# Block-sparse attention and feed-forward on one core: three score banks instead of two, and squares kept in their place

## The chip, the cores and the metric

One core of a Trainium2 chip runs the kernel. Its engines work side by side: PE multiplies matrices, DVE, ACT and POOL work on vectors, and SP issues the transfers. The metric is the time of one execution in microseconds.

## What is computed

Attention with 4 batches, 8 heads, 768 positions and 64 numbers per head, followed by a feed-forward layer on the 3072 tokens that come out of it:

```python
scores = scale * np.matmul(q, k.transpose(0, 1, 3, 2))
mask = np.abs(blk_i - blk_j) <= window          # blocks of 32
mask = mask | (blk_i == 0) | (blk_j == 0) | (blk_i == n_blocks - 1) | (blk_j == n_blocks - 1)
...                                             # and three sampled blocks for each block of q
scores = np.where(mask, scores, -1000000000.0)
attn = np.exp(scores - np.max(scores, axis=-1, keepdims=True))
attn = attn / (np.sum(attn, axis=-1, keepdims=True) + 1e-09)
x = np.matmul(attn, v)                          # tokens x 512
h = x @ w_in                                    # 512 -> 2048
out = np.maximum(0.01 * h, h) @ w_out           # 2048 -> 512
```

Since each block of q sees at most twelve blocks of keys (two blocks of q together), the kernel gathers these keys and values and computes 384 scores per row.

## The kernel before

The work is cut into 192 units: twelve items (batch b and pair of query tiles j), in each four groups of queries k and four pairs of heads hp. A tile of the unit 3, 2, 1, 0 is named s_3_2_1_0, and so on. A unit goes through this chain. PE multiplies q by the gathered keys into a PSUM bank s (line 651), DVE adds the mask and takes the extreme into mx (658), ACT takes the exponential (669), DVE makes the reciprocal r of the sums (677, 678), ACT writes the high fp16 half of the weights into pp (684), DVE the low half (689), SP issues the transpose of pp into pt (692), PE multiplies pt by the gathered values vg into the bank av (714), and ACT, DVE and POOL turn that into the input x of the feed-forward (721 to 732). pp and pt have six buffers each.

The feed-forward is cut into 96 chunks. For each, 24 matmuls fill a bank h (749), ACT (756) and DVE (760) read it, and DVE and POOL write g (765, 766). Twelve matmuls multiply g by the second weight into the bank o (779), ACT writes ob (797), and SP issues the output (808). The bank h is free again once DVE's line 760 has read it.

Queries and keys are split into high and low halves before use. prep_q squares a tile of q on ACT (523) with a sum per row, one small matmul of PE adds the rows up (126, q_sum), DVE makes the scale, ACT writes the high half of qa (530), DVE the low one (532), SP issues the transpose into qs (535), and two copies of it with the two halves of the partitions swapped into qxs (537, 538). The load of the next q into the single buffer rq is line 473. prep_k does the same for keys (494, 126, 506, 508, transpose 512); from the second batch on, the four head pairs of a batch share one buffer k16, so that the square of a pair writes where the transpose of the pair before still reads.

The gathered values vg are copied from DRAM by SP: one copy of 128 rows (611) and six of 32 rows (621), whose addresses SP loads and computes first (619). All transfers of the kernel, loads, transposes, gathers and outputs, are issued on SP, in one order.

PSUM has eight banks: two for s, three with the tag h (these also hold the small sums), one for av, two for o.

The main loop goes through the units, and the letters of a string set in which order the pieces of work of a step are written. A scheduler then orders the instructions of each engine by priority. The priority is a running number; the helper together lowers it for all but the first matmul of a group, so that a group stays in one piece. Scores are written one step ahead, for two units at once when the first of a pair of units is done (the setting spair), and the second unit of the pair comes first on PE. An instruction without a late priority can be placed ahead of others on its engine as soon as the scheduler believes its inputs to be there; the squares of prep_q and prep_k and their matmuls are such.

Of the kernel before, what the change touches and what calls it, by code (L numbers as in the profile page):

```python
# [13 lines left out]
F32 = mybir.dt.float32  # L14
# [5 lines left out]
P = 128  # L20
# [9 lines left out]
CFG = {  # L30
    "ahead": 3,
    "av_lag": 3,
    "bs": 1500,
    "early": 2,
    "flag": 1,
    "g": 2,
    "g_at": 0,
    "ht": 1,
    "k_at": 6,
    "k_at0": 26,  # L40
# [10 lines left out]
    "rk": 2,  # L51
    "rmax": 1.0,
    "rmin": 0.0,
    "side": 1.2,
    "side0": 1.6,
    "spair": 1,
    "spread": 8,
    "v_at": 28,
    "wr": [(0, 1.0), (4, 3.0), (10, 4.0), (18, 4.5)],
# [6 lines left out]
def tile_block_sparse_attention_ffn(  # L66
# [19 lines left out]
    nc = tc.nc  # L86
# [20 lines left out]
    pa = ctx.enter_context(tc.tile_pool(name="pa", bufs=2))  # L107
    pf = ctx.enter_context(tc.tile_pool(name="pf", bufs=2))
    dr = ctx.enter_context(tc.tile_pool(name="dr", bufs=2, space=bass.MemoryType.DRAM))
    ps_s = ctx.enter_context(tc.tile_pool(name="ps_s", bufs=2, space=bass.MemoryType.PSUM))  # L110
    ps_o = ctx.enter_context(tc.tile_pool(name="ps_o", bufs=2, space=bass.MemoryType.PSUM))
    ps_1 = ctx.enter_context(tc.tile_pool(name="ps_1", bufs=1, space=bass.MemoryType.PSUM))

# [1 line left out]
    nc.vector.memset(zero, 0.0)  # L115

    def bank(name, tag="h"):
        return ps_1.tile([P, 512], F32, tag=tag, name=name, bufs={"h": 3, "av": 1}[tag])


    ones = cst.tile([P, P], F32, name="ones")
# [2 lines left out]
    def scale_sum(ss, n, name):  # L124
        pb = bank(f"{name}_sum")
        nc.tensor.matmul(pb[:, :n], ones, ss, start=True, stop=True)
        return pb

    def scale_of(pb, n, name, total=False, keep=None, fl="q"):

        pool, tg = (sm, "sc") if keep is None else (cst, keep)
        m = 1 if total else n
        tot = sm.tile([P, 4], F32, tag=f"tot{fl}", name=f"{name}_tot")
        if total:
            nc.vector.tensor_reduce(out=tot[:, :1], in_=pb[:, :n], op=ALU.add, axis=AX.X)
            nc.vector.tensor_scalar(out=tot[:, :1], in0=tot[:, :1], scalar1=TINY, scalar2=None, op0=ALU.max)
        else:
            nc.vector.tensor_scalar(out=tot[:, :m], in0=pb[:, :m], scalar1=TINY, scalar2=None, op0=ALU.max)  # L140
        ex = sm.tile([P, 4], I32, tag=f"ex{fl}", name=f"{name}_ex")
        nc.vector.tensor_scalar(
            out=ex[:, :m], in0=tot[:, :m].bitcast(I32), scalar1=24, scalar2=23,
            op0=ALU.logical_shift_right, op1=ALU.logical_shift_left,
        )
        inv = pool.tile([P, 4], F32, tag=f"{tg}_i", name=f"{name}_inv")
        s = pool.tile([P, 4], F32, tag=f"{tg}_s", name=f"{name}_s")
        nc.vector.tensor_scalar(out=inv[:, :m], in0=ex[:, :m].bitcast(F32), scalar1=2.0 ** 50, scalar2=None, op0=ALU.mult)
        nc.vector.reciprocal(out=s[:, :m], in_=inv[:, :m])
        return inv, s  # L150
# [3 lines left out]
    def scales(ss, n, name, **how):  # L154
        now = tc.cur_priority
        tc.cur_priority = now - CFG["bs"]
        begin = len(nc.cur_bb.bb.instructions)
        pb = scale_sum(ss, n, name)
        loose.update(i.name for i in nc.cur_bb.bb.instructions[begin:])
        r = scale_of(pb, n, name, **how)  # L160
        tc.cur_priority = now + 8
        return r

    def together(emits):

        now = tc.cur_priority
        begin = len(nc.cur_bb.bb.instructions)
        for n, emit in enumerate(emits):
            if n == 1:
                tc.cur_priority = now - 100000  # L170
            emit()
        new = nc.cur_bb.bb.instructions[begin:]
        for i in new[1:]:
            tc.add_manual_dep(i, new[0].name, mybir.DependencyInfo(
                mybir.DependencyClass.NoSync, mybir.DependencyReason.DATA), reason="together")
        tc.cur_priority = now + len(new)
# [40 lines left out]
    def build_masks():  # L217
# [8 lines left out]
        for r in range(NR):  # L226
# [9 lines left out]
            pattern=[[-1, NB - 2], [0, NR]], base=-1, channel_multiplier=1,  # L236
            compare_op=ALU.is_equal, fill=0.0)
        pm = bank("mask_ps")[:, :(NT - 1) * 2 * NR].rearrange("p (t a r) -> p t a r", t=NT - 1, a=2)
        for a in range(2):
            sel = sels[a]  # L240
# [244 lines left out]
    def prep_k(b, hp, rk):  # L485

        nm = f"k{b}_{hp}"
        ss = sm.tile([P, 1], F32, tag="ssk", name=f"ss_{nm}")
        if b == 0:
            k16 = early_k.bitcast(F16)[:, (NP + hp) * 2 * S:(NP + hp + 1) * 2 * S].rearrange(  # L490
                "p (n l d) -> p n l d", n=HC, l=2)
        else:
            k16 = pa.tile([P, HC, 2, D], F16, tag="k16", name=f"k16_{nm}", bufs=1)
        nc.scalar.activation(flat(k16)[:, :S], flat(rk), AF.Square, accum_out=ss)
        yield 1.0
        yield 0.01
        pb = scale_sum(ss, 1, nm)
        yield 0.2
        inv, s = scale_of(pb, 1, nm, fl="k")
        if (b, "inv") not in kready:  # L500
            kready[b, "inv"] = cst.tile([P, NP], F32, name=f"kinv_{b}")
        nc.vector.tensor_scalar(
            out=kready[b, "inv"][:, hp:hp + 1], in0=inv[:, :1], scalar1=-SCALE, scalar2=None, op0=ALU.mult)
        yield 0.4
        raw = rk.rearrange("p h c d -> p (h c) d")
        nc.scalar.activation(k16[:, :, 1, :], raw, AF.Copy, scale=s[:, :1])
        yield 1.0
        nc.vector.scalar_tensor_tensor(
            out=k16[:, :, 0, :], in0=raw, scalar=s[:, :1], in1=k16[:, :, 1, :], op0=ALU.mult, op1=ALU.subtract)
        if b not in kts:  # L510
            kts[b] = pa.tile([P, H, S], F16, tag="kt", name=f"kt_{b}", bufs=2)
        nc.sync.dma_start_transpose(
            out=kts[b][:, 2 * hp:2 * hp + 2, :].rearrange("p h (c t) -> p (h c) t", t=P),
            in_=k16.rearrange("p n l d -> p (n l d)"))
        kready[b, hp] = True
        yield 1.2

    def prep_q(b, j, i, rq):

        nm = f"q{b}_{j}_{i}"  # L520
        ss = sm.tile([P, 1], F32, tag="ssq", name=f"ss_{nm}")
        qa = pa.tile([P, H, 2, D], F16, tag="qa", name=f"qa_{nm}", bufs=1)
        nc.scalar.activation(flat(qa)[:, :H * D], rq.rearrange("p h d -> p (h d)"), AF.Square, accum_out=ss)  # L523
        yield 0.7
        yield 0.01
        pb = scale_sum(ss, 1, nm)
        yield 0.2
        inv, s = scale_of(pb, 1, nm)
        yield 0.4
        nc.scalar.activation(qa[:, :, 1, :], rq, AF.Copy, scale=s[:, :1])  # L530
        yield 0.7
        nc.vector.scalar_tensor_tensor(
            out=qa[:, :, 0, :], in0=rq, scalar=s[:, :1], in1=qa[:, :, 1, :], op0=ALU.mult, op1=ALU.subtract)
        qs = pa.tile([P, H, P], F16, tag="qs", name=f"qs_{nm}", bufs=2)
        nc.sync.dma_start_transpose(out=qs, in_=flat(qa))
        qxs = pa.tile([P, H, P], F16, tag="qxs", name=f"qxs_{nm}", bufs=2)
        nc.sync.dma_start(out=qxs[:D], in_=qs[D:])
        nc.sync.dma_start(out=qxs[D:], in_=qs[:D])
        qstack[b, j, i] = (qs, qxs, inv)
        yield 0.8  # L540
# [157 lines left out]
    def pair_av(pr):  # L698

        if pr.hp == 0:  # L700
            avs[pr.item.n, pr.T] = bank(f"av_{pr.nm}", "av").rearrange("p (n l t) -> p n l t", n=NP, l=2)
        pr.av = avs[pr.item.n, pr.T]
        for u in pr.units:
            require_v(u.b, u.hp, u.T)
        emits = []
        for u in pr.units[::-1]:
            n = NCH * u.parts
            for c in range(n):
                for l in range(2):
                    for hh in range(2):  # L710
                        vt = vgs[u.b, u.T][:, c, 2 * u.hp + hh, :] if u.T else v16s[u.b, u.hp][:, c, hh, :]
                        emits.append(lambda o=pr.av[hh * D:(hh + 1) * D, u.hp], a=vt[:, l * D:(l + 1) * D],
                                     m=u.pt[c // NCH][:, :, c % NCH, hh * D:(hh + 1) * D], c=c, l=l, n=n:
                                     nc.tensor.matmul(o, a, m, start=(c == 0 and l == 0), stop=(c == n - 1 and l == 1)))  # L714
        together(emits)

    def tile_evac(pr):

# [93 lines left out]
    for b in range(B):  # L812
        for j in range(NI):
# [3 lines left out]
            for k_ in range(TPI):  # L817
                for hp in range(0, NP, 2):
                    pr = Unit()
# [30 lines left out]
    def require_v(b, hp, T):  # L850
        until(("v", b), lambda: (b, hp) in v16s if T == 0 else (b, "ready") in scr)
        while T and (b, T) not in vgs:
            start_gather_v()
# [173 lines left out]
    for u in units:  # L1027
        it, ui = u.item, u.k * NP + u.hp
        b, nb = it.b, it.b + 1
# [161 lines left out]
```

## Time and profile before

| what | time, us |
|---|---|
| median of three runs | 949.08 |
| lowest and highest | 946.14 and 949.32 |
| the profiled execution | 946.47 |
| its span | 944.7 |
| PE busy in it | 754.8 |
| DVE busy | 609.1 |
| ACT busy | 488.1 |
| POOL busy | 331.3 |

The profile counts an engine as busy while it computes. SP computes nothing, so it does not stand in this table; what it does is seen in its timeline, where each row is the time during which SP worked on issuing transfers. A wait in the list of waits is idle time of an engine ahead of an instruction, put down to the instruction or transfer that came last. Windows give the busy time of each engine in a stretch and the clock that was granted to PE.

### The profile page before, as it was taken

To read this page: it belongs to the slowest core of one execution; us is meant where nothing else is said; L and a number is where in the kernel's file an instruction comes from. 1 tells how busy PE (TensorE), PEld (TensorE's weight loads), DVE (VectorE), ACT (ScalarE), POOL (GpSimd) and SP (SyncE) were. 2 spreads that over 40 slices of the span, in tenths; PEclk is the share of its full clock that TensorE was granted. 3 is DMA by queue.
4 is the path that set the end of the run, shared out by engine and by line. 5 is a ranking of instruction groups with operands and counts; after the bars stand their busy time and mean duration, and the time that the engine had idled before them with its cause. 6 is when DMAs were issued, how large, how long until landed. Compare 5 with 4: busy or idle time off the path is not lost. (4 is left out here: it accounts for less than half of the span.)

```text
span 944.7 us, 21784 instructions
## 1 busy us (share of the span) xinstructions
PE 754.8 (80%) x7020; PEld 492.8 (52%) x7020; DVE 609.1 (64%) x1643; ACT 488.1 (52%) x1063; POOL 331.3 (35%) x469
## 2 busy tenths in 40 slices
PE   1325456788978979979897968989888988989998
PEld 1214334465645645646554635556455655656674
DVE  4989899996857667557565565567466655745221
ACT  4565768575535456456455554456355554535121
POOL 0234665542215344243324242333323433532221
PEclk9998557799989989999999998999999999989999
DMA  9996798678685767766675978676785665555200
GB/s 209 283 276 162 162 244 187 164 148 167 141 180 128 160 121 157 160 137 130 151 165 111 171 134 147 151 146 127 151 161 125 137 136 139 120 113 123 32 23 23
DMA packets 336624, 139.38 MB, mean 148 GB/s; under 512 B 299389, under 2 KB 311678, under 8 KB 336510
## 3 DMA queue, kind: packets, MB, share of 16 engines
q1 hardware_dynamic: 336510, 137.99, 68.5%
q8 instruction: 55, 0.90, 0.4%
q14 instruction: 59, 0.48, 0.2%
HBM read 65.57 MB, written 12.58 MB: 83 GB/s over the span
## 5 line engine op out<-in xcount | busy, mean ns | idle before, releaser
L779 PE MATMUL o<-W,g 128*128 128x512 f16 x1152 | 279.1, 388 | 7.6 <-ACT ob L797 2.9
L749 PE MATMUL h<-x,W 128*128 128x256 f16 x2304 | 280.9, 279 | 0.3 <-DVE ht L760 0.3
L749 PEld LDWEIGHTS <-W 128*128 128x128 f16 x2304 | 227.2, 101 | 50.7 <-issue 10.5
L766 POOL TENSOR_TENSOR g<-ht,g 128x512 f16<-128x512 f32 x96 | 115.3, 1201 | 336.5 <-DVE g L765 201.2
L689 DVE SCALAR_TENSOR_TENSOR pp<-p,r,pp 128x384 f16<-128x384 f32 x208 | 142.5, 702 | 106.0 <-ACT pp L684 104.4
L779 PEld LDWEIGHTS <-g 128*128 128x128 f16 x1152 | 108.8, 100 | 137.4 <-issue 23.9
L669 ACT ACTIVATE p<-p,mx 128x384 f32<-128x384 f32 x208 | 125.8, 606 | 96.3 <-DVE mx L658 67.0
L591 POOL COPY kg<-kt 128x256 f16 x264 | 129.3, 510 | 131.6 <-PE s L651 74.9
L684 ACT ACTIVATE pp<-p,r 128x384 f16<-128x384 f32 x208 | 119.6, 607 | 103.9 <-DMA pt<-pp 72.0
L714 PE MATMUL av<-pt,vg 128*64 128x128 f16 x2112 | 83.0, 231 | 50.5 <-DMA pt<-pp 40.3
L658 DVE CUSTOM_DVE_ANT_0 p<-s,em,nsc 128x384 f32<-128x384 f32 x176 | 101.9, 609 | 21.1 <-PE s L651 20.0
L714 PEld LDWEIGHTS <-vg 128*64 128x64 f16 x2112 | 72.1, 116 | 77.0 <-issue 57.4
L760 DVE SCALAR_TENSOR_TENSOR ht<-h,gd,ht 128x512 f32<-128x512 f32 x80 | 59.8, 747 | 56.0 <-ACT ht L756 55.7
L756 ACT ACTIVATE ht<-h,gs 128x512 f32<-128x512 f32 x80 | 54.0, 675 | 63.9 <-PE h L749 48.7
L651 PE MATMUL s<-kg,qs_q 128*64 128x384 f16 x352 | 65.1, 364 | 12.1 <-DVE mx L658 7.7
L732 POOL TENSOR_TENSOR x<-xf,x 128x256 f16<-128x256 f32 x48 | 35.8, 745 | 90.7 <-ACT x L730 90.0
L651 PE MATMUL s<-kg,qxs_q 128*64 128x384 f16 x352 | 63.9, 357 | 4.3 <-DMA qxs_q<-qs_q 4.3
L651 PEld LDWEIGHTS <-qs_q 128*64 128x64 f16 x416 | 27.9, 116 | 68.7 <-issue 45.4
L523 ACT ACTIVATE qa_q<-rq 128x512 f16<-128x512 f32 x25 | 15.7, 628 | 68.9 <-DMA rq<-in_q_dram 68.9
L765 DVE CAST g<-ht 128x512 f16<-128x512 f32 x96 | 43.4, 452 | 8.9 <-PE o L779 7.5
L677 DVE TENSOR_SCALAR sum<-sum 128x2 f32<-128x2 f32 x96 | 24.9, 259 | 37.1 <-ACT p L669 36.1
L669 ACT ACTIVATION_READ_ACCUMULATOR p<-p,mx 128x1 f32 x208 | 38.9, 187 | 0.0
(126 smaller groups left out, 726.0 us busy)
## 6 DMA issues: line engine op xcount, KB each, us to landing
vg<-scr SPq DMA_DIRECT2D x280, 64.0 KB, 1.9
vg<-scr SPq DMA_DIRECT2D x44, 256.0 KB, 3.1
v<-in_v_dram SPq DMA_DIRECT2D x32, 192.0 KB, 3.4
qxs_q<-qs_q SPq DMA_DIRECT2D x48, 128.0 KB, 3.0
scr<-v SPq DMA_DIRECT2D x16, 384.0 KB, 3.7
W<-in_moe_w_in_dram SPq DMA_DIRECT2D x5, 1024.0 KB, 5.9
rq<-in_q_dram SPq DMA_DIRECT2D x20, 256.0 KB, 3.5
out_dram<-ob SPq DMA_DIRECT2D x20, 256.0 KB, 2.3
```

What stands on the lines that cost most here:

```text
L591: nc.gpsimd.tensor_copy(out=kg[:, :, slot * BLOCK:(slot + 1) * BLOCK], in_=kt[:, :, bass.ds(off, BLOCK)])
L651: nc.tensor.matmul(o, a, k, start=(n == 0), stop=(n == 1)))
L658: nc.vector.tensor_tensor_reduce(out=u.p[i], in0=u.sp[i], in1=kgs[u.b, u.T][1] if u.T else zero.to_broadcast([P, KEYS]), scale=u.nsc, scal ...
L669: nc.scalar.activation(u.p[i], u.p[i], AF.Exp, scale=-1.0, bias=u.mx[:, :1], accum_out=u.pair.sum[:, u.pi, i:i + 1])
L684: nc.scalar.activation(pp[:, 0, :], p, AF.Copy, scale=u.r)
L689: nc.vector.scalar_tensor_tensor(out=pp[:, 1, :], in0=p, scalar=u.r, in1=pp[:, 0, :], op0=ALU.mult, op1=ALU.subtract)
L714: nc.tensor.matmul(o, a, m, start=(c == 0 and l == 0), stop=(c == n - 1 and l == 1)))
L749: nc.tensor.matmul(c.ph[:, i], w, x, start=(d == 0 and m == 0), stop=(d == NP - 1 and m == 2)))
L756: nc.scalar.activation(c.t, c.ph, AF.Copy, scale=scale[1])
L760: nc.vector.scalar_tensor_tensor(out=c.t, in0=c.ph, scalar=scale[0], in1=c.t, op0=ALU.mult, op1=ALU.max)
L766: nc.gpsimd.tensor_tensor(out=c.g[:, 1], in0=c.t, in1=c.g[:, 0], op=ALU.subtract)
L779: nc.tensor.matmul(o, a, w, start=(c.first and i == 0 and m == 0), stop=(c.last and i == 1 and m == 2)))
```

## The change

Three banks instead of two for s, and two instead of three with the tag h. Scores are written for one unit at a time, in the order of the units (spair 0). And a new helper, hold, ties an instruction to the one that stands before it on the same engine in the written program, without a wait on the chip: only the order of the engine is fixed. It is applied to the square and the sum matmul of every k but those of the first batch, and of every q but the very first. A third use, for av, stays off.

```diff
+    "hold": "kq",
+    "s": 3,
-    "spair": 1,
+    "spair": 0,
-    ps_s = ctx.enter_context(tc.tile_pool(name="ps_s", bufs=2, space=bass.MemoryType.PSUM))
+    ps_s = ctx.enter_context(tc.tile_pool(name="ps_s", bufs=CFG["s"], space=bass.MemoryType.PSUM))
-        return ps_1.tile([P, 512], F32, tag=tag, name=name, bufs={"h": 3, "av": 1}[tag])
+        return ps_1.tile([P, 512], F32, tag=tag, name=name, bufs={"h": 5 - CFG["s"], "av": 1}[tag])
+    def hold(begin):
+
+        ins = nc.cur_bb.bb.instructions
+        prev = next((i for i in reversed(ins[:begin]) if i.engine == ins[begin].engine), None)
+        if prev is not None:
+            tc.add_manual_dep(ins[begin], prev.name, mybir.DependencyInfo(
+                mybir.DependencyClass.NoSync, mybir.DependencyReason.DATA), reason="hold")
...
+        begin = count()
         nc.scalar.activation(flat(k16)[:, :S], flat(rk), AF.Square, accum_out=ss)
+        if b and "k" in CFG["hold"]:
+            hold(begin)
         yield 1.0
         yield 0.01
+        begin = count()
         pb = scale_sum(ss, 1, nm)
+        if b and "k" in CFG["hold"]:
+            hold(begin)
...
+        later = (b or j) and "q" in CFG["hold"]
+        begin = count()
         nc.scalar.activation(flat(qa)[:, :H * D], rq.rearrange("p h d -> p (h d)"), AF.Square, accum_out=ss)
+        if later:
+            hold(begin)
         yield 0.7
         yield 0.01
+        begin = count()
         pb = scale_sum(ss, 1, nm)
+        if later:
+            hold(begin)
```

In the rows that follow, numbers at the end of a name are buffers' numbers, and the same statement has another line number after the change.

ACT, at the preparation of q2_1_1, whose high half is `qa_q2_1_1`. Before, the high half came five rows ahead of the square of k3_2:

```order
L506 ACTIVATE k16_k3_1_10014<-rk_3_1_9666,k3_1_s_10282 128x12x64
L684 ACTIVATE pp_2_1_1_0_0_10656<-p_2_1_1_0_0_10462,r_2_1_1_0_10647 128x384
L756 ACTIVATE ht_1_2_10_10344<-h_1_2_10_10306,gs2_2849 128x512
L669 ACTIVATE p_2_1_1_2_0_10650,sum_2_1_1_2_10658<-p_2_1_1_2_0_10650,mx_2_1_1_2_10651 128x384
L669 ACTIVATE p_2_1_1_3_0_10709,sum_2_1_1_2_10658<-p_2_1_1_3_0_10709,mx_2_1_1_3_10710 128x384
L530 ACTIVATE qa_q2_1_1_10148<-rq_2_1_1_9664,q2_1_1_s_10392 128x8x64
L684 ACTIVATE pp_2_1_1_1_0_10715<-p_2_1_1_1_0_10496,r_2_1_1_0_10647 128x384
L721 ACTIVATE avt_2_0_3_2_10678<-av_2_0_3_0_10429 128x256
L684 ACTIVATE pp_2_1_1_2_0_10771<-p_2_1_1_2_0_10650,r_2_1_1_2_10762 128x384
L730 ACTIVATE x_2_0_9710<-xf_2_0_3_2_10732 128x4x64
L494 ACTIVATE k16_k3_2_10457,ss_k3_2_10456<-rk_3_2_10113 128x768
```

And now:

```order
L524 ACTIVATE k16_k3_1_10014<-rk_3_1_9666,k3_1_s_10277 128x12x64
L709 ACTIVATE pp_2_1_1_1_0_10715<-p_2_1_1_1_0_10496,r_2_1_1_0_10642 128x384
L749 ACTIVATE avt_2_0_3_2_10678<-av_2_0_3_0_10424 128x256
L709 ACTIVATE pp_2_1_1_2_0_10766<-p_2_1_1_2_0_10645,r_2_1_1_2_10757 128x384
L758 ACTIVATE x_2_0_9705<-xf_2_0_3_2_10727 128x4x64
L784 ACTIVATE ht_1_2_10_10344<-h_1_2_10_10301,gs2_2844 128x512
L507 ACTIVATE k16_k3_2_10452,ss_k3_2_10451<-rk_3_2_10108 128x768
L709 ACTIVATE pp_2_1_1_3_0_10835<-p_2_1_1_3_0_10709,r_2_1_1_2_10757 128x384
L555 ACTIVATE qa_q2_1_1_10148<-rq_2_1_1_9664,q2_1_1_s_10392 128x8x64
```

The high half of q2_1_1 now stands two rows behind the square of k3_2, which writes where the transpose of k3_1 reads.

SP, at the same place: from the transpose of k3_1 to that of q2_1_1, before:

```order
L692 DMA_TRANSPOSE pt_2_1_0_0_0_10408<-pp_2_1_0_0_0_10340 128x6x128
L512 DMA_TRANSPOSE kt_3_10011<-k16_k3_1_10014 128x12x128
L535 DMA_TRANSPOSE qs_q2_1_1_10397<-qa_q2_1_1_10148 128x8x128
L473 DMA rq_2_2_0_10402<-in_q_dram 128x8x64
L692 DMA_TRANSPOSE pt_2_1_0_1_0_10466<-pp_2_1_0_1_0_10410 128x6x128
```

And now:

```order
L717 DMA_TRANSPOSE pt_2_1_0_0_0_10408<-pp_2_1_0_0_0_10335 128x6x128
L530 DMA_TRANSPOSE kt_3_10011<-k16_k3_1_10014 128x12x128
L717 DMA_TRANSPOSE pt_2_1_0_1_0_10461<-pp_2_1_0_1_0_10410 128x6x128
L494 DMA rk_3_3_10493<-in_k_dram 128x6x64 x2
L717 DMA_TRANSPOSE pt_2_1_0_2_0_10500<-pp_2_1_0_2_0_10463 128x6x128
L636 DMA vg0_95<-scr_2_8209 128x1024
L644 TENSOR_LOAD offs_89
L644 ISA x2
L646 ISA
L646 DMA vg0_95<-scr_2_8209 32x1024
L560 DMA_TRANSPOSE qs_q2_1_1_10397<-qa_q2_1_1_10148 128x8x128
```

Two transposes of pp, two loads of k and two copies to vg have come in between. At the last q, q3_2_1, the rows of SP (row 1465 of 1540 before, 1466 of 1541 now) have the same neighbours in the same order as before.

PE, behind the sum of the last q (row 11981 of 13879 before and now), before:

```order
L126 MATMUL q3_2_1_sum_15945<-ss_q3_2_1_15739,ones_83 128x1
L651 LDWEIGHTS qs_q3_2_0_15274
L651 MATMUL s_3_2_1_1_0_15979<-kg1_94,qs_q3_2_0_15274 64x384
L651 LDWEIGHTS qs_q3_2_0_15274
L651 MATMUL s_3_2_1_1_0_15979<-kg1_94,qs_q3_2_0_15274 64x384
L651 LDWEIGHTS qxs_q3_2_0_15276
L651 MATMUL s_3_2_1_1_0_15979<-kg1_94,qxs_q3_2_0_15276 64x384
L651 LDWEIGHTS qxs_q3_2_0_15276
L651 MATMUL s_3_2_1_1_0_15979<-kg1_94,qxs_q3_2_0_15276 64x384
L651 LDWEIGHTS qs_q3_2_0_15274
L651 MATMUL s_3_2_1_0_0_15978<-kg1_94,qs_q3_2_0_15274 64x384
```

And now:

```order
L128 MATMUL q3_2_1_sum_15945<-ss_q3_2_1_15739,ones_83 128x1
L676 LDWEIGHTS qs_q3_2_0_15274
L676 MATMUL s_3_2_1_0_0_15978<-kg1_94,qs_q3_2_0_15274 64x384
L676 LDWEIGHTS qs_q3_2_0_15274
L676 MATMUL s_3_2_1_0_0_15978<-kg1_94,qs_q3_2_0_15274 64x384
L676 LDWEIGHTS qxs_q3_2_0_15276
L676 MATMUL s_3_2_1_0_0_15978<-kg1_94,qxs_q3_2_0_15276 64x384
L676 LDWEIGHTS qxs_q3_2_0_15276
L676 MATMUL s_3_2_1_0_0_15978<-kg1_94,qxs_q3_2_0_15276 64x384
L739 LDWEIGHTS vg1_96
L739 MATMUL av_3_1_3_0_15987<-pt_3_1_3_1_0_15710,vg1_96 64x128
```

The scores of one unit stand there where those of two stood, and the first unit comes first.

## Rows read from the trace of the kernel before

**Rows 1.** Busy time by stretch: stretch, length, engines, PE clock, DMA share, GB/s.

```profile
150.00:769.00 619.00, 532.80 (x5075) 344.93 (x5073) 411.86 (x1144) 331.85 (x754) 219.37 (x332) 0.95 0.71 147
769.00:840.00 71.00, 67.94 (x660) 44.85 (x655) 44.27 (x115) 35.22 (x83) 29.41 (x45) 0.98 0.58 128
```

**Rows 2.** Timeline of SP, 759 to 776: start, length, line, operation, how many.

```profile
759.81 6.04 SPq L621 DMA_DIRECT2D vg<-scr  x6
765.95 3.90 SPq L692 DMA_TRANSPOSE pt<-pp  x3
769.94 1.26 SPq L535 DMA_TRANSPOSE qs_q<-qa_q  x1
```

**Rows 3.** Tile pp from 0 to 760 us: instructions, first and last start.

```profile
L689 DVE SCALAR_TENSOR_TENSOR pp<-p,r,pp x180: 594/618/2475, 53.0 to 759.2; 128x384 f16<-128x384 f32 x180
L692 SPq DMA_TRANSPOSE pt<-pp x175: 1209/1252/3559, 59.7 to 756.9; - x175
```

**Rows 4.** Waits, whole run (last row: 150 to 880 us): total, times, longest.

```profile
ACT pp L684 <- DMA pt<-pp: 72.0, 33, 6.8
ACT qa_q L523 <- DMA rq<-in_q_dram: 68.9, 20, 6.3
...
PE av L714 <- DMA pt<-pp: 54.7, 29, 5.3
...
PE s L651 <- DVE mx L658: 25.4, 11, 9.6
...
PE k_sum L126 <- ACT k_k L494: 20.8, 7, 4.9
...
PE s L651 <- DVE mx L658: 4.4, 5, 1.3
```

**Rows 5.** Waits of SP's own queue, whole run: three of its rows.

```profile
SPq L537 <- DMA qs_q<-qa_q: 6.1, 8, 2.3
SPq L512 <- DVE W L314: 4.5, 1, 4.5
...
SPq L535 <- DVE W L312: 3.4, 1, 3.4
```

**Rows 6.** Timelines of ACT, DVE and SP around q2_1_1, 555 to 573 us.

```profile
561.54 0.70 ACT L530 ACTIVATE qa_q<-rq,q_s 128x512 f16<-128x512 f32 x1
...
568.63 0.84 ACT L494 ACTIVATE k_k<-rk 128x768 f16<-128x768 f32 x1 [2.42 <-DMA kt<-k_k]
...
562.27 0.75 DVE L532 SCALAR_TENSOR_TENSOR qa_q<-rq,q_s,qa_q 128x512 f16<-128x512 f32 x1 [0.24 <-ACT qa_q L530]
...
563.75 1.45 SPq L512 DMA_TRANSPOSE kt<-k_k  x1
565.29 1.62 SPq L535 DMA_TRANSPOSE qs_q<-qa_q  x1
...
570.76 1.32 SPq L482 DMA_DIRECT2D rk<-in_k_dram  x1
```

**Rows 7.** Timelines of SP and PE at the last q, 836 to 850 us.

```profile
839.49 1.27 SPq L535 DMA_TRANSPOSE qs_q<-qa_q  x1
...
842.82 0.51 PE L651 MATMUL s<-kg,qs_q 128*64 128x384 f16 x3 [1.60 <-DMA qs_q<-qa_q]
845.97 0.82 PE L651 MATMUL s<-kg,qxs_q 128*64 128x384 f16 x3 [2.63 <-DMA qxs_q<-qs_q]
```

**Rows 8.** Line 749: the page's row, its share by stretch, one chunk's timelines.

```profile
L749 PE MATMUL h<-x,W 128*128 128x256 f16 x2304 | 280.9, 279 | 0.3 <-DVE ht L760 0.3
...
769.00:846.00 77.00, 28.24 (x240) 22.82 (x240) 0.97 0.59 130
...
460.04 2.76 PE L779 MATMUL o<-W,g 128*128 128x512 f16 x12
462.64 2.78 PE L749 MATMUL h<-x,W 128*128 128x256 f16 x24
...
472.51 0.74 DVE L760 SCALAR_TENSOR_TENSOR ht<-h,gd,ht 128x512 f32<-128x512 f32 x1
```

More of the change, by code (lines that the diff above doesn't have):

```diff
@@ L162, in scales @@
         return r
+    def hold(begin):
[4 more added lines that the diff above has]
+                mybir.DependencyClass.NoSync, mybir.DependencyReason.DATA), reason="hold")
+    count = lambda: len(nc.cur_bb.bb.instructions)
     def together(emits):
@@ L714, in pair_av @@
                                      nc.tensor.matmul(o, a, m, start=(c == 0 and l == 0), stop=(c == n - 1 and l == 1)))
+        begin = count()
         together(emits)
+        if pr.item.n and "a" in CFG["hold"]:
+            hold(begin)
     def tile_evac(pr):
```

## The prediction, made before the changed kernel ran

> **What bounds the kernel now.** I read the share of busy time by stretch first. Between 150 and 769 us PE is busy 532.80 of 619 us, and between 769 and 840 it is busy 67.94 of 71 us [rows 1]. A reader might stop there and call PE the bound, with some 86 us of idle time in the long middle stretch to be won by a better order. The next view, the DMA issues on SP, says otherwise. Every DMA of this kernel is issued on that one queue, and its rows lie end to end: six gathers from 759.81 for 6.04 us end at 765.85, three transposes of pp start at 765.95 and take 3.90 us, to 769.85, the transpose of qs starts at 769.94 [rows 2]. One transpose of pp holds SP for 1.252 us, and 175 of them start before 760 us [rows 3], 219 us in all; a gather step costs about 6.04/6 = 1.01 us. SP has no room in which to go faster.
>
> Whether SP or its producers are behind is told by counting. By 760 us DVE has finished 180 tiles of pp and SP has taken up 175 of them [rows 3]: five finished tiles, some 6 us of transposes, are lying in front of SP. pp has six buffers, so this is nearly as far ahead as the producers can get. Hence the large waits in the list are SP's lag seen from other engines: ACT waits 72.0 us for a transpose that would free a pp buffer, PE 54.7 us for pt, ACT 68.9 us for the next q [rows 4]. All of these end with something that SP issues.
>
> The end is set so. SP issues the transpose of the last q (q3_2_1) at 839.49; PE runs out of other scores, waits 1.60 us for it at 842.82 and 2.63 us for its swapped copy at 845.97 [rows 7], and then has work without a real pause to the end at 944.7. So the time is SP's row count up to that transpose, plus some 99 us of PE work behind it.
>
> **The change, part by part.** The sum starts from the profiled run, 946.47 us (span 944.7 and 1.8 around it). The three runs had a median of 949.08, 2.6 above this one, and it was itself near their low end.
>
> SP's own rows: the same transposes, gathers and loads. The transpose of the last q stands at row 1465 before and 1466 now, between the same neighbours, so the pace-setter has the same work ahead of the critical point: 0 us. What SP itself waits is small. It waits 6.1 us for qs ahead of the swapped copies, 4.5 and 3.4 us at the start for transposes whose tiles come behind the decoding of the weights [rows 5]; 14 us in all, the most that a new order could take from SP. The swapped copies still follow their transpose at a distance of one to six rows, so I take 0 and keep -14 for the range.
>
> Scores, one unit at a time with three banks: no matmul is added or removed. The waits that it aims at, PE's scores on DVE's read of the last bank, are 25.4 us in 11, of which only 4.4 us in 5 lie between 150 and 880 us [rows 4]; the other 21 are at the start, while SP issues loads. I put this at 0, since the freed PE would only bring pp sooner to a queue that already has five tiles lying. If that cover were missing, it is -4.4.
>
> Squares held in place (ACT and PE): a q square comes 8 to 20 rows later on ACT, so ACT waits less in front of it for its load, and the matmul behind a k square no longer stands early on PE, where such matmuls cost 20.8 us of waiting [rows 4]. Again 0 for the time, covered by SP; -20.8 without the cover. The reverse side is one place where SP itself comes to depend on ACT. At q2_1_1 the high half on ACT started at 561.54 and the low half on DVE at 562.27, ending at 563.02; SP wanted them at 565.29 [rows 6]. Now the high half stands behind the square of k3_2, and this square waits for the transpose of k3_1, issued at 563.75, to leave the buffer; it started at 568.63 [rows 6]. Add the square's 0.84, 0.7 for one pp, and 0.70 and 0.75 for the two halves: ready at about 571.6. SP reaches the moved transpose after two pt (2.5), two loads of k (1.32) [rows 6] and two copies to vg (1.5 by the gather steps): 563.75 + 1.45 + 5.3 = 570.5. So SP stands some 1.1 us, with all pt behind it: **+1.1**. It is 0 if SP is a little later there than I count, and 5.5 if ACT in front of the high half waits twice for a pp buffer as long as it does on average, 72.0/33 = 2.2 us [rows 4].
>
> Feed-forward with two banks instead of three: with three, PE waited 0.3 us for a bank in the whole run [rows 8]. A bank is free when DVE has read it. In the long case h ended at 462.64 + 2.78 = 465.42 and DVE's read at 472.51 + 0.74 = 473.25, 7.8 us later [rows 8]. With two banks the next but one product waits if PE has less than that to do between. One other h (2.78 us) and one o (2.76) make 5.5 [rows 8], so the long case costs 2.3 us. Ten products lie between 769 and 846 (240 matmuls of 24 each) [rows 8]; there PE has 1.60 + 2.63 = 4.2 us to give before it, not SP, sets the end. Earlier than 769 the five tiles in front of SP cover it. Bounds: 0 if no release is long, 10 x 2.3 - 4.2 = +19 if every one is. In the busy middle ACT and DVE also serve attention, as they do at 465; towards the end they are freer. I take two long ones, 4.6 against 4.2 of slack: **+0.4**, and use five long ones, 11.5 less 4.2 = +7.3, for the rival below and the range.
>
> The sum: 946.5 + 0 + 1.1 + 0.4 = 948.0 on the level of the profiled run. A median of several runs may lie there or, as it did before, 2.6 higher; I add 1 and forecast **949**: no change.
>
> Two rules of the Trainium skill bear on this. Its page Perfetto Trace Analysis says under What "DMA-bound" means that a kernel can be bound by the issuing engine's sequencer, which then shows solid DMA slices. The trace agrees: three groups of SP rows in a row have at most 0.10 us between them [rows 2]. By that rule a reordering of PE and ACT alone leaves 946.5. The same page asks under Matmuls that independent groups rotate through different PSUM banks, so that one's evacuation overlaps the next; taking a bank from the feed-forward goes against it, and by it the time would be the second rival's.
>
> **The rivals.** *PE sets the pace.* If the queue in front of SP were a mere consequence of bursts, PE's own waits would count: 20.8 for the k sums and 4.4 for the scores [rows 4]: 946.5 - 25.2 = 921.3, some 923 for a median. For it speaks PE's 68 of 71 us between 769 and 840; against it, SP's rows without gaps and the tiles lying in front of it at 760. Chance 0.10.
>
> *Two banks are too few.* The mechanism above with five long releases between 769 and 846: 948.0 - 0.4 + 7.3 = 955. It decides from the second long release on, where 4.2 us are used up. For it: PE is busy 96% there. Against: with three banks only one wait of 0.3 us was seen. This ends slower. Chance 0.14.
>
> *SP waits for ACT.* What I priced at 1.1 us at q2_1_1 comes at further q's too, since the high halves now stand later on ACT while SP wants them at the same place. Three more places, at each of which ACT waits its average 2.2 us for a pp buffer [rows 4] ahead of the high half: +6.6, from 948.0 to 955. It decides once a high half comes later than SP's own lag of some 6 us covers. Chance 0.11.
>
> *SP's own waits shrink.* If the start, where attention comes some rows sooner past the weight decoding, gives SP its 4.5 and 3.4, and half of the 6.1 goes: 7.9 + 3.1 = 11 less than 948.0 is 937, with the same 1 added 938. Chance 0.17.
>
> That the hold does nothing for k is possible as well: its square stays 11 to 16 rows from the transpose it waits for. It would give the forecast's time and is counted in it.
>
> **How the numbers follow.** Forecast 0.48, rivals 0.10, 0.14, 0.11 and 0.17. About 0.5% (4.7 us) is what measurement tells from no change: under 944.3 faster, over 953.8 slower. Faster 0.10 + 0.17 = 0.27, slower 0.14 + 0.11 = 0.25, same 0.48. The forecast's own range is 944.5 to 953.5. For 8 in 10 I leave out PE's pace (0.10), the lowest part of SP's waits and what lies above 958, together some 0.18: 936 to 958.
>
> **What would show it.** In the changed kernel's trace: SP's rows still end to end from 60 to 878 us; finished pp still ahead of taken ones at 760; the last q's transpose issued within 5 us of 839.5; some 99 us behind it. The score waits on DVE and the k sums' waits gone without SP moving would prove the cover; waits of h on DVE at L760's place between 769 and 846 the second rival; a semaphore wait of SP before a qs transpose the third. The forecast is wrong if SP shows gaps where before it had none, or if that transpose is issued before 834.

## The result, and the profile after

The changed kernel takes 952.08 us against 948.99 for the kernel before, in 15 runs each: a ratio of 1.0043, interval 1.0028 to 1.0057 (the ratio is worked out over all runs; the quotient of the two medians is 1.0033). Three later comparisons gave 1.0089 (1.0068 to 1.0110), 1.0058 (1.0035 to 1.0081) and 1.0061 (1.0038 to 1.0084). It is slower by 4 to 8 us. The time lies inside the forecast's range, but the forecast was no change, and that is wrong. The time lies between the forecast and the second and third rival, both at 955; what the runs show is the mechanism of neither.

The head of the page of after: span and busy time by engine.

```profile
span 949.1 us, 21876 instructions
...
PE 758.9 (80%) x7020; PEld 493.3 (52%) x7020; DVE 604.0 (64%) x1643; ACT 491.4 (52%) x1063; POOL 323.5 (34%) x469
```

PE and ACT are busy 4.1 and 3.3 us longer than before, DVE and POOL less long. The list of waits of after (total, times, longest), which answers to [rows 4]:

```profile
ACT pp L709 <- DMA pt<-pp: 84.2, 48, 4.4
...
PE av L739 <- DMA pt<-pp: 57.3, 29, 7.8
...
PE s L676 <- DVE mx L683: 25.5, 16, 6.6
...
PE s L676 <- DMA qs_q<-qa_q: 25.5, 8, 8.8
...
PE k_sum L128 <- ACT k_k L507: 8.3, 4, 2.9
...
ACT qa_q L543 <- DMA rq<-in_q_dram: 3.2, 1, 3.2
```

What the holds aim at is mostly gone: ACT waits 3.2 us for the next q instead of 68.9, PE 8.3 us for the k squares instead of 20.8. The waits for pt stay (57.3 against 54.7 on PE, 84.2 against 72.0 on ACT), and PE now waits 25.5 us for a transposed q (12.5 before, and 20.5 in e1 below, which costs nothing). Scores still wait 25.5 us for DVE, as before (25.4).

The end, from the timelines of SP and PE of after; it answers to [rows 7]:

```profile
844.06 1.28 SPq L560 DMA_TRANSPOSE qs_q<-qa_q  x1
...
847.39 0.35 PE L676 MATMUL s<-kg,qs_q 128*64 128x384 f16 x2 [0.40 <-DMA qs_q<-qa_q]
850.55 0.53 PE L676 MATMUL s<-kg,qxs_q 128*64 128x384 f16 x2 [2.81 <-DMA qxs_q<-qs_q]
```

The last q's transpose is issued at 844.06 instead of 839.49, 4.57 us later, and the span is 949.1 instead of 944.7, 4.4 longer. Behind the transpose lie 105.0 us, before it was 105.2. So everything was lost on the way to this transpose, and nothing behind it. In every trace of this study 103 to 106 us lie behind it:

| run | ratio to before (interval) | span of the trace | last q's transpose issued | from there to the end |
|---|---|---|---|---|
| before | | 944.7 | 839.49 | 105.2 |
| the change | 1.0043 (1.0028 to 1.0057) | 949.1 | 844.06 | 105.0 |
| e1 banks only | 0.9997 (0.9967 to 1.0027) | 952.4 | 847.40 | 105.0 |
| e2 hold only | 1.0131 (1.0099 to 1.0163) | 955.3 | 851.02 | 104.3 |
| e3 banks, k held | 1.0003 (0.9978 to 1.0027) | 945.5 | 840.60 | 104.9 |
| e4 banks, q held | 1.0004 (0.9989 to 1.0019) | 943.9 | 839.13 | 104.8 |
| e5 the change | 1.0089 (1.0068 to 1.0110) | 951.5 | 846.60 | 104.9 |
| e6 more on SP | 1.0266 (1.0238 to 1.0294) | 969.2 | 866.47 | 102.7 |
| e7 less on SP | 0.9972 (0.9949 to 0.9995) | 943.5 | 838.05 | 105.5 |
| e8 the change, less on SP | 0.9958 (0.9931 to 0.9984) | 944.4 | 841.02 | 103.4 |
| e9 five squares free | 1.0001 (0.9977 to 1.0026) | 947.6 | 842.83 | 104.8 |
| e10 two squares free | 1.0004 (0.9982 to 1.0025) | 944.6 | 838.60 | 106.0 |
| e11 the change | 1.0058 (1.0035 to 1.0081) | 952.3 | 847.41 | 104.9 |
| e12 banks, less on SP | 0.9930 (0.9902 to 0.9957) | 936.7 | 831.94 | 104.8 |
| e13 only 2_1_1 free | 1.0081 (1.0057 to 1.0105) | 953.7 | 847.64 | 106.1 |
| e14 the change | 1.0061 (1.0038 to 1.0084) | 945.6 | 840.83 | 104.8 |

A trace shows one run, and the runs of one kernel lie some 4 to 8 us to either side of their median (e1: 940.4 to 954.5). The trace of e1 is of one of its longest runs, that of e14 of one of the shortest of the change. So ratios come from the timed runs, and what is read from traces below is read from several.

### The profile page after: what moved, and what is told of

Its sections match the earlier page's. It is cut to its first block, busy times and chain, and to the rows that moved or that the text cites. A ratio compares the mean times of both kernels' runs of the same rounds, so it can differ in the third digit from the quotient of the medians.

```text
span 949.1 us, 21876 instructions
## 1 busy us (share of the span) xinstructions
PE 758.9 (80%) x7020; PEld 493.3 (52%) x7020; DVE 604.0 (64%) x1643; ACT 491.4 (52%) x1063; POOL 323.5 (34%) x469
## 5 line engine op out<-in xcount | busy, mean ns | idle before, releaser
L714 DVE SCALAR_TENSOR_TENSOR pp<-p,r,pp 128x384 f16<-128x384 f32 x208 | 145.6, 712 | 95.8 <-ACT pp L709 95.1
L616 POOL COPY kg<-kt 128x256 f16 x264 | 124.9, 492 | 185.7 <-PE s L676 128.2
L709 ACT ACTIVATE pp<-p,r 128x384 f16<-128x384 f32 x208 | 120.4, 607 | 117.3 <-DMA pt<-pp 84.2
L807 PEld LDWEIGHTS <-g 128*128 128x128 f16 x1152 | 107.0, 99 | 139.8 <-issue 25.5
L683 DVE CUSTOM_DVE_ANT_0 p<-s,em,nsc 128x384 f32<-128x384 f32 x176 | 105.1, 611 | 64.1 <-PE s L676 62.6
L739 PE MATMUL av<-pt,vg 128*64 128x128 f16 x2112 | 85.6, 234 | 47.7 <-DMA pt<-pp 38.7
L676 PEld LDWEIGHTS <-qxs_q 128*64 128x64 f16 x416 | 26.1, 120 | 16.1 <-DMA qxs_q<-qs_q 10.0
```

The source lines that it names most:

```text
L616: nc.gpsimd.tensor_copy(out=kg[:, :, slot * BLOCK:(slot + 1) * BLOCK], in_=kt[:, :, bass.ds(off, BLOCK)])
L676: nc.tensor.matmul(o, a, k, start=(n == 0), stop=(n == 1)))
L683: nc.vector.tensor_tensor_reduce(out=u.p[i], in0=u.sp[i], in1=kgs[u.b, u.T][1] if u.T else zero.to_broadcast([P, KEYS]), scale=u.nsc, scal ...
L709: nc.scalar.activation(pp[:, 0, :], p, AF.Copy, scale=u.r)
L714: nc.vector.scalar_tensor_tensor(out=pp[:, 1, :], in0=p, scalar=u.r, in1=pp[:, 0, :], op0=ALU.mult, op1=ALU.subtract)
L807: nc.tensor.matmul(o, a, w, start=(c.first and i == 0 and m == 0), stop=(c.last and i == 1 and m == 2)))
```

## Which part of the change costs the time

The first four kernels take the change apart.

e1 keeps the banks and the single units and drops all holds:

```diff
-    "hold": "kq",
+    "hold": "",
```

> Three score banks, one unit at a time, two banks for h; no instruction is held. The 3 us that the whole change costs are lost on SP before the last q's transpose (issued at 844.06 instead of 839.49), not behind it. If the holds are the cause (theory A), this kernel takes 949 like the kernel before and that transpose is issued near 839.5. If the banks are the cause (theory B), it takes 952 and the transpose is issued near 844. If each brings half (theory C), 950.5.

Measured: 0.9997. The banks cost nothing and bring nothing. Theory B falls.

e2 keeps the holds and goes back to the old banks:

```diff
-    "s": 3,
-    "spair": 0,
+    "s": 2,
+    "spair": 1,
```

> The squares of q and k and their sums held in place, with the old banks (two for scores in pairs, three for h). Theory A (the holds cost it): 952, last q's transpose near 844. Theory B (the banks): 949 and 839.5. The waits of ACT for rq (68.9 us) and of PE for the k squares (20.8 us) fall in both theories, and the time does not follow them.

Measured: 1.0131, 10 us slower by the medians and 12 by the ratio, where theory A expected 3. The place is at the start. In SP's order the transpose of the third q (0_1_0) stands at row 115 here, at 101 in the kernel before and at 105 in the whole change. SP's timeline of e2 there:

```profile
93.60 1.83 SPq L316 DMA_DIRECT2D W<-in_moe_w_in_dram  x2
95.55 9.65 SPq L717 DMA_TRANSPOSE pt<-pp  x4
...
107.90 3.90 SPq L560 DMA_TRANSPOSE qs_q<-qa_q  x1
```

and of the kernel before, at the same q:

```profile
80.03 5.25 SPq L692 DMA_TRANSPOSE pt<-pp  x4
...
90.73 1.27 SPq L535 DMA_TRANSPOSE qs_q<-qa_q  x1
```

Four transposes behind two loads of weights hold SP for 9.65 us instead of 5.25, and the transpose of q takes 3.90 instead of 1.27. So a row of SP does not always cost the same. What lengthens it is not shown: loads of weights stand ahead of it here, but in the kernel before four transposes behind loads of v and k took 8.90 us:

```profile
59.72 8.90 SPq L692 DMA_TRANSPOSE pt<-pp  x4
```

This loss is that of the holds with the old banks. The whole change does not have it there: up to 246 us its SP is, in the mean of three traces, within 1.0 us of the mean of the kernels that cost nothing (counted as below).

e3 and e4 hold only k, or only q, with the new banks:

```diff
-    "hold": "kq",
+    "hold": "k",
```

> The whole change without the hold of q: only the squares of k are held. If the hold of q makes the loss (its transposes come later among SP's rows, next to k's), 949; if that of k, 952; if neither, the time of the banks alone.

> The whole change without the hold of k: only the squares of q are held. If the hold of q makes the loss, 952; if that of k, 949; if neither, the time of the banks alone. ACT's wait for rq falls here as in the whole change.

Measured: 1.0003 and 1.0004. With the new banks neither hold costs anything by itself. e4 also has ACT's wait for the next q gone (3.0 us are left), at no gain. What is left is a cost that only the two holds together have.

## Does SP set the pace?

e6 gives SP 44 more address computations, with the kernel before:

```diff
+            if slot == 6:
+                nc.sync.value_load(offs[:1, i:i + 1], min_val=0, max_val=S - BLOCK)
             off = nc.sync.value_load(offs[:1, i:i + 1], min_val=0, max_val=S - BLOCK)
```

> The kernel before, with one more load and computation of a gather address on SP for each of the 44 gathers (about 0.27 + 0.15 us and the pauses between, some 0.65 us each, 42 of them ahead of the last q's transpose). If SP's queue sets the pace: +27 us, 976. If PE's own waits set it and SP has room: 949.

Measured: 971.02 against 945.36, 25.7 us more where 27 were expected. What is added to SP is added to the time.

e7 and e8 take 48 loads away from SP, from the kernel before and from the changed one:

```diff
-            nc.sync.dma_start(out=t[:, h], in_=k[b, 2 * hp + h]...
+            (nc.scalar if b else nc.sync).dma_start(out=t[:, h], in_=k[b, 2 * hp + h]...
-            nc.sync.dma_start(out=t[:, :, h, :], in_=v[b, 2 * hp + h]...
+            (nc.scalar if b else nc.sync).dma_start(out=t[:, :, h, :], in_=v[b, 2 * hp + h]...
```

> The kernel before, with the loads of k and v of batches 1 to 3 issued on ACT instead of SP (48 rows of SP less, about 20 us for k and 14 for v, with the pauses some 36). If SP's queue sets the pace: 913. If PE does: 949, or slower by what ACT loses.

> The changed kernel with the same loads on ACT. If SP still sets the pace, 913 to 917, the same as the kernel before with this edit. If SP is relieved so far that PE's waits count, the change shows its gain here: up to 25 us (the waits of scores and k sums) under the kernel before with this edit.

Measured: 0.9972 and 0.9958. Both expectations miss: of some 36 us taken from SP, 3 to 4 come out. The tile pp of e7 from 0 to 760 us (instructions, first and last start) answers to [rows 3]:

```profile
L689 DVE SCALAR_TENSOR_TENSOR pp<-p,r,pp x180: 593/618/2553, 57.9 to 756.7; 128x384 f16<-128x384 f32 x180
L692 SPq DMA_TRANSPOSE pt<-pp x177: 1209/1252/3295, 59.6 to 757.1; - x177
```

Three finished tiles lie in front of SP instead of five (averaged over 150 to 800 us, 3.1 instead of 3.7), and the producers have made no more of them: 180 by 760 us, as before. SP's rows, fewer now, are broken by waits, of which the longest are 4.6 us at 93 and 4.8 us at 185 us.

Where the relief went can be added up on SP, from the start to the issue of the last q's transpose: the lengths of its rows (transfers and address computations), the waits (more than 0.25 us between two rows) and the short pauses. The loads of k and v took 38.2 us before and 6.3 in e7, 31.9 less. SP's other rows took 18.6 us more (690.8 against 672.2), and its waits grew from 19.9 to 33.5. So adding to SP costs its full length, and relieving it brings almost nothing: more than half of the relief went into longer rows, the rest into waits. The waits fit producers that run at nearly SP's pace, but e7 does not prove it: the 48 issues take 26.9 us on ACT, which makes pp, and a version that takes rows off SP without giving them to ACT was not run. What bounds the producers then is not settled here. In e8 the change costs nothing against e7 (0.9958 and 0.9972, intervals that overlap).

## Where the two holds cost together

In the orders of SP, one thing belongs to the whole change alone: the transposes of some q's stand later than with one hold or none. For q 1_1_1 it is row 571 against 559 to 562, for 2_1_1 row 947 against 936 to 940. These are the places where a k square is held as well, so that the high half of q comes behind it, as the prediction described for 2_1_1.

> The whole change once more, beside the kernel before on the chip of this call. The banks alone, the banks with the hold of k, and the banks with the hold of q all took the time of before, so that the whole change should cost nothing if its parts add (theory A: 0 us, as forecast). If the two holds only cost together (theory B), it is 3 to 4 us slower here too, and the last q's transpose is issued about 4 us later than in the kernel before. In both theories the end comes 105 us after that issue.

Measured: 1.0089, 954.06 against 945.36. The loss is real, theory B.

e9, e10 and e13 free the squares of some q's, and leave all else held:

```diff
-        later = (b or j) and "q" in CFG["hold"]
+        later = (b or j) and "q" in CFG["hold"] and (b, j, i) not in {(1, 1, 1), (2, 1, 1)}
```

> The whole change, but five squares of q (1_0_0, 1_0_1, 1_1_1, 2_0_1, 2_1_1) are not held. In the order of SP, only the whole change has the transposes of four of these q's 9 to 13 rows later than any other variant (1_0_1 at row 448 instead of 435, 1_1_1 at 571 instead of 562, 2_0_1 at 817 instead of 810, 2_1_1 at 947 instead of 940); here they stand at 440, 562, 810 and 940. If the late transposes are the loss (theory A), this kernel takes the time of before, 0 to 2 us above it. If the loss is spread over all held squares (theory B), most of it stays: 5 us or more above.

> The whole change, but only the squares of q 1_1_1 and 2_1_1 are not held: the places where a held k square stood ahead of the high half of q. Their transposes return to SP's rows 561 and 939; those of 1_0_0 (398) and 1_0_1 (448) stay late. If these two places are the loss: the time of before. If the two late q's at the start of batch 1 carry it: as slow as the whole change.

> The whole change once more, in the same call as the two kernels with freed squares, so that they can be set beside it: 3 to 8 us above the kernel before, last q's transpose at 844 to 847.

Measured side by side: 1.0001, 1.0004, and 1.0058 for the change. Freeing two squares out of 22 takes the whole loss away.

> The whole change, but only the square of q 2_1_1 is not held: its transpose returns to row 940 of SP's order, that of q 1_1_1 stays late, at row 571 instead of 561. The mean of three traces of the change lies 0.4 us ahead of the trace of before on SP at 315 us, 2.8 behind at 406, 4.0 behind at 518 and 4.2 at 805. If the place at 1_1_1 (363 us) carries the loss (theory A): 5 us above the kernel before, as the whole change. If it takes the place at 2_1_1 (575 us) or both (theory B): 0 to 2 us above.

> The whole change beside it, on the same chip: 3 to 8 us above the kernel before.

Measured: 1.0081 with only 2_1_1 free, 1.0061 for the change. So the hold of the square of q 1_1_1 brings the loss, and freeing 2_1_1, where the prediction had looked, does not help. (Of the 24 q's the two of the first item are not held, which leaves 22. Freeing 1_1_1 alone gives the same order of SP, PE, DVE and POOL as e10, and a slightly different one of ACT; it was not run, and e10 stands for it.)

The place itself. ACT and DVE of after, 357 to 363 us:

```profile
358.36 0.84 ACT L507 ACTIVATE k_k<-rk 128x768 f16<-128x768 f32 x1 [0.34 <-DMA kt<-k_k]
...
361.08 0.72 ACT L555 ACTIVATE qa_q<-rq,q_s 128x512 f16<-128x512 f32 x1 [1.28 <-DVE q_s L151]
...
361.84 0.75 DVE L557 SCALAR_TENSOR_TENSOR qa_q<-rq,q_s,qa_q 128x512 f16<-128x512 f32 x1
```

SP of after, from the k load to the copies of q (start, length):

```profile
357.66 1.16 SPq L494 DMA_DIRECT2D rk<-in_k_dram  x2
358.92 1.21 SPq L717 DMA_TRANSPOSE pt<-pp  x1
360.23 0.52 SPq L636 DMA_DIRECT2D vg<-scr  x1
361.74 1.47 SPq L646 DMA_DIRECT2D vg<-scr  x2
363.31 1.26 SPq L560 DMA_TRANSPOSE qs_q<-qa_q  x1
364.62 0.57 SPq L485 DMA_DIRECT2D rq<-in_q_dram  x1
366.50 0.50 SPq L562 DMA_DIRECT2D qxs_q<-qs_q  x1
```

and of e10, with the square of 1_1_1 free:

```profile
356.89 0.58 SPq L494 DMA_DIRECT2D rk<-in_k_dram  x1
357.57 1.23 SPq L560 DMA_TRANSPOSE qs_q<-qa_q  x1
358.84 0.61 SPq L485 DMA_DIRECT2D rq<-in_q_dram  x1
359.50 0.64 SPq L494 DMA_DIRECT2D rk<-in_k_dram  x1
360.24 1.80 SPq L717 DMA_TRANSPOSE pt<-pp  x1
362.13 0.54 SPq L562 DMA_DIRECT2D qxs_q<-qs_q  x1
```

The held square of k2_2 runs first, the high half of q starts at 361.08 instead of 355.94, and the transpose goes out at 363.31 instead of 357.57. SP does not wait for the halves: they are ready at 362.59. It waits one step later. The swapped copies need the transpose to have landed. In e10 a load of k and a transpose of pp lie between, beside the load of the next q, and cover that. In the change both have already been issued, only the load of the next q is left (to 365.19), and SP stands until 366.50: 1.26 us without its rows' usual short pauses. The same gap is in all five traces with the late row (e13: from 366.98 to 368.27) and, at this q, not in before, e1, e3, e4, e9 or e10.

It is tempting to call this gap the loss. Three readings speak against it. First, e8 has the late row and a gap of 1.3 us at the same q, and costs nothing against e7. Second, gaps like it stand at other q's in kernels that cost nothing. The kernel before has one at q 0_1_0 (load of the next q, then the first copy):

```profile
92.06 0.57 SPq L473 DMA_DIRECT2D rq<-in_q_dram  x1
93.97 0.51 SPq L537 DMA_DIRECT2D qxs_q<-qs_q  x1
```

and in sum SP waits ahead of the copies for 4.1 to 8.1 us in the five late traces and for 3.6 to 8.2 us in the six others. Two of the rows, of e14 and of e3 (total, times, longest):

```profile
SPq L562 <- DMA qs_q<-qa_q: 4.1, 6, 1.2
...
SPq L562 <- DMA qs_q<-qa_q: 7.9, 11, 1.6
```

Third, the gap is made up. The change and e10 have the same rows of SP in the same order up to 358 us, then differ at this transpose, and again in 18 stretches between 429 and 820 us. Where both have issued the same set of rows, their times can be set side by side. At the load of k that opens the lists above, the four traces of the change are in the mean 0.7 us behind e10, at 376 us 0.5, and at this copy of v, in after and in e10, 1.2:

```profile
487.05 0.57 SPq L465 DMA_DIRECT2D scr<-v  x1
...
486.09 0.57 SPq L465 DMA_DIRECT2D scr<-v  x1
```

At the last q's transpose they are 6.1 us behind. From the load of k to the copy of v the single traces lose 0.2 to 0.9 us on e10, and from there to the last q 3.2 to 6.1. Against e9, whose trace is of one of its longer runs, the four differences are 0.3, 0.5, 0.5 and 1.9. So the place itself leaves about half a microsecond, and most of the loss comes after 487 us.

How much is lost, and where, can be counted on SP. I added up the median lengths (from the trace of before) of what SP has done, and took how much the clock has run ahead of that sum; this grows with stretched rows and with waits. Over the 460 us of SP's work from 240 to 700, it grows by 51.4, 51.4, 52.6, 53.8 and 49.8 us in the five traces with the late row (after, e5, e11, e13, e14; mean 51.8), and by 47.1, 47.6, 46.2, 49.4 and 47.8 in before, e3, e4, e9 and e10 (mean 47.6). The difference is 4.2 us, or 3.4 with e1 among the latter (its trace, of one of its longest runs, grows by 52.6). By this count 3.0 of the 4.2 come between 240 and 340 us of work, 293 to some 406 us on the clock (12.5 against 9.5); but it sets orders beside each other that differ, and against e10, row by row, what is behind at 403 us (1.75) is half made up at 436 (0.9). Just before 403 stands a copy that is longer in the late traces: the first copy of the next gather takes 1.11 us in after,

```profile
398.47 1.11 SPq L636 DMA_DIRECT2D vg<-scr  x1
```

1.66 to 1.70 us in the four other traces with the late row, and 0.53 to 0.58 in before, e1, e3, e4, e9 and e10. This is half a microsecond to one more. What stretches this copy is not shown.

The sums of SP say what kind of time was lost. Up to the last q's transpose, the same rows took 714.7, 715.5, 720.0, 718.5 and 713.2 us in the five late traces (mean 716.4), and 710.4, 715.4, 710.6, 710.8, 710.2 and 712.6 us in before, e1, e3, e4, e9 and e10 (mean 711.7). The waits were 20.5 and 20.8 us in the mean, the short pauses 108.4 and 108.8. So in the mean SP does not wait longer in the change; the same rows take it 4.7 us longer. Single traces scatter, in their waits from 17.0 (e10) to 24.3 us (e9), so this says where the time goes on average and not in any one run. The excess is spread over the kinds of rows: the largest parts are 1.7 us on the transposes of pp and 1.5 on those of q.

What stays open: by which path the held square makes later rows longer. Freeing it also changes the order behind it, on SP in the 18 stretches named above, so that the late transpose is not separated from the order that comes with it; a kernel with the square free and the transpose alone moved late was not run.

## A version that is faster than both

e12 takes the banks of the change without any hold, and issues the 48 loads on ACT:

> Three score banks without any hold, and the loads of k and v of batches 1 to 3 issued on ACT. The held version with these loads on ACT was 0.4% under the kernel before. If the banks gain once SP has room: 4 us or more under the kernel before. If what gained there was the hold (ACT no longer waits for q's load): the time of before.

Measured: 939.14 against 946.84, 0.9930 (0.9902 to 0.9957), while the change, run beside it, took 952.51. The last q's transpose goes out at 831.94. The same loads on ACT gave 0.9972 with the old banks (e7) and 0.9958 with the whole change (e8), in another comparison, with intervals that overlap this one. So whether it is the banks that gain once SP has room, and whether the hold takes from it, stays open. That e12 beats both kernels is measured.

## The prediction, point by point

**SP and 99 us behind it: right, and only half of it.** The end follows the issue of the last q's transpose by 102.7 to 106.1 us in all sixteen traces (the 99 us count from PE's start on the swapped copy, 845.97), and 27 us put on SP cost 25.7. But the prediction took SP's time as the count of its rows, and e7 shows that 48 rows fewer do not make it shorter by their length.

**Waits that vanish without gain: right.** ACT's 68.9 us for q fell to 3.2, the k sums' 20.8 to 8.3, and the time did not fall. The first rival, PE's pace at 923, is refuted.

**Scores in three banks, 0: right** (e1, 0.9997). The score waits on DVE did not even fall.

**Two banks for h, +0.4: right in that nothing is lost behind 769 us.** In after PE waits for no bank of h in that stretch; its waits there are nearly all for the transposed q. The second rival falls.

**SP's own waits, 0 with -14 as the bound: right.** Its waits add up to 20.5 us in the mean of the five late traces against 20.8 in the six others. The fourth rival falls.

**SP's own rows, the same work, so 0: the step that failed.** The transpose of the last q stands at row 1466 instead of 1465, and the prediction took from this that SP reaches it at the same time. SP issued it 4.57 us later in after, and the time grew by 4 to 8 us. The same rows took SP 716.4 us in the mean of the five late traces instead of 711.7, with no more waiting in the mean. That a row's length varies could be read beforehand, from 1.209 to 3.559 us for one form of transpose [rows 3]; the term counted rows at their median. What brings it here is the hold of the square of q 1_1_1 together with that of k (e10 and e13); why the rows behind it get longer stays open.

**SP waits for ACT, +1.1: right in kind at its place, and not the loss.** The prediction priced it at 2_1_1. There the halves were ready at 574.90 and SP, which had stood for 0.36 us, issued at 574.93; the change's other traces have 0.43 to 0.49 us there. e13 shows that freeing this place does not help. At the sister place 1_1_1, which the prediction did not look at, SP came after the halves were ready, and waited for the landing of the transpose instead, a wait that was made up. The third rival, at 955, comes near in number, but its mechanism, SP waiting longer, is not what the sums show.

## What to carry to other kernels

When one queue sets the pace, the number of its rows is not its time: the same rows took it 710 to 720 us here, depending on the order and the run. A gap that appears where the order was changed is not yet the loss. Set the rows of the two kernels side by side further on, and add up the waits of the whole queue, before calling it the cause; here the gap was made up ten microseconds later. Look at every place of a pattern: freeing the place that had been priced changed nothing, and freeing its sister as well took the whole loss away. And before calling a queue the bound, ask both questions: adding to it and taking from it gave quite different answers.

## What the runs showed of the hardware that was not expected

The time for which a DMA issue holds its queue is not fixed: a transpose of pp takes 1.252 us at the median and 3.559 at the longest [rows 3], and behind two loads of weights the mean of four was 2.4 us and a transpose of q took 3.90. Up to the last q's transpose the same rows held SP for 710.2 to 720.0 us in eleven traces, and for 713.2 to 720.0 us in the four with the whole change, whose order is the same. Taking 31.9 us of loads off the queue (e7) made its other rows 18.6 us longer. What lengthens a row is not shown by any run here.
